# K as whole pairs in three shared slots in layers 1 and 2, and another order at a layer's end, in four attention layers of one decode step

## The chip, the cores and the metric

The kernel runs on one core of a Trainium2 chip. The metric is device time in microseconds, the median of several executions. A profile is one execution, taken by the hardware profiler, with its own time.

## What is computed

One token passes through four attention layers. Layers 1 and 3 use the weights and caches A, layers 2 and 4 those of B; everything is bfloat16.

```python
D, H, Sk, Dh = 640, 32, 8192, 192
def attn(x, k_cache, v_cache, wq, wo):
    q = (x @ wq) as [32 heads, 192]
    scores = einsum("hd,hkd->hk", q, k_cache) * Dh ** -0.5
    p = softmax(scores)
    o = einsum("hk,hkd->hd", p, v_cache)
    return o.reshape(1, 32 * 192) @ wo
x = x + attn(layernorm(x), A...)
x = x + attn(layernorm(x), B...)
x = x + attn(layernorm(x), A...)
x = x + attn(layernorm(x), B...)
```

K and V of one layer are 201 MB. Each byte is used for one query only, so nearly all of the 845 MB that are read are read once.

## The kernel before, in words

**Pairs, halves, slots.** In the code layers are counted 0 to 3; the text says layer 1 to 4. Heads go in 16 pairs (`NPAIR`). The K (or V) of a pair is 128 partitions x 24,576 values, 6144 KB, and consists of two halves of 12,288 values. `pool` in SBUF has eight slots (`NSLOT`), each as large as a half. Slots 5 to 7 (from `A_WQ`) hold A's query weights until layer 3. In layers 1 and 2 five slots are left: K's half 0 lies in slot 0, half 1 in slot 1, a pair's V in slots 2 and 3 as one transfer, and output weights, or a half of pair 15's K, in slot 4.

**Work on a pair.** `products` (L714) multiplies a K half in place by the query, which VectorE (DVE) does in chunks of columns (L729), and TensorE (PE) sums the products over the head dimension with matmuls by the identity, 24 a half, into a bank of `S` (one bank a half; L744, and L72 where the weights stay loaded). In layers 1 and 2 a half has two chunks of 96 columns for pairs 2 to 13, and four of 48 else. `softmax` (L778) reads both banks, `values` (L804) multiplies by V on PE (L841, L72), `gather` (L851) adds up the groups on DVE (L865, L867) and writes a row. The steps of a pair are m (half 0), m (half 1), s, v, e; every fifth pair also projects a block of output weights.

**Order.** `steps` is the order of work on the engines, `plan` the order of transfers. All large transfers are issued by SyncE (SP) in the order of `plan`, in one queue, on 16 DMA engines; each of them carries 8 of the 128 partitions, so a transfer has 16 landings, and the last one counts. `allot` (L345) gives a transfer its slots and notes in `before` whose work it waits for; `joint` lists the pairs that go as one transfer (`whole`, L242; issued at L464, others at L467). `transfer` (L426) waits on SyncE for the PE instruction after which the slots are free. What stands behind a waiting transfer waits too.

**A layer's end.** Pairs 14 and 15 come as halves. Pair 15's half 0 of K goes to slot 4 and half 1 to slot 0; then the last block of output weights into slot 4 (waits for that half 0), V15's first half into slot 1 and its second into slot 0, in layer 2 with its last part apart (`vq`) and two rows of weights apart (`wob`). In layer 1 the weights are issued before V15's halves too (`plan.insert(-2, ...)`, L302). The next layer's query weights take slots 2 to 4. Layer 3 starts with K in quarters (`kp`), the first of which waits for the projection of layer 2's last block.

Of the kernel before, what the change touches and what calls it, by code (L numbers as in the profile page):

```python
# [77 lines left out]
PAIRS_W = 5  # L78
# [4 lines left out]
def build(nc, A_x, A_k, A_v, A_wq, A_wo, B_x, B_k, B_v, B_wq, B_wo, out):  # L83
# [31 lines left out]
    with ExitStack() as ctx:  # L115
# [14 lines left out]
        K0Q = slot[NSLOT - 1][:, TS // 2:]  # L130
        QUARTER = [K0Q, slot[A_WQ - 1][:, TS // 2:], slot[A_WQ - 1][:, 0:TS // 2], slot[A_WQ][:, 0:TS // 2]]
        KEYS = [0, 2, 1, 3]
        CUT = NB[1] * D
        PIECE = [(0, TS // 2, K0Q), (TS // 2 + CUT, 3 * TS // 2, slot[A_WQ - 1][:, CUT:]),
                 (TS // 2, TS // 2 + CUT, slot[A_WQ - 1][:, 0:CUT]), (3 * TS // 2, 2 * TS, QUARTER[3])]
# [103 lines left out]
        def stays(kind, l, p):  # L239
            return l < 2 and (kind, pair(l, p)) in KEPT[l]  # L240

        def whole(kind, l, p):  # L242

            if l < 2:
                return (kind, l, p) in joint
            if kind == "k":
                return l == 3 and p > 1
            if p == NPAIR - 1:
                return False
            return l != 2 or p not in (0, PAIRS_W, 2 * PAIRS_W)  # L250
# [7 lines left out]
        for l in range(NL):  # L258
            if l < 3:
                plan += [("wq", l, 0), ("wq", l, 2)][:(1, 2, 0)[l]]  # L260
                ahead_of = [{0: (0, DC)}, {0: (0, DC - 1), 2: (DC - 1, DC)}, {0: (0, 1), 2: (1, DC)}][l]
                for c in ([0, 2, 3, 1, 4] if l == 2 else range(DC)):
                    steps += [("lead", l, 0, *ahead_of[c])] if c in ahead_of else []
                    steps.append(("r", l, c))
            else:
                both(("wq", l, 0))
            for p in range(NPAIR):
                if l == 0 and p == 0:
                    plan.append(("kh", l, p))
                if l == 2 and p == 0:  # L270
                    plan += [("kp", l, p, i) for i in range(1, len(PIECE))]
                else:
                    plan += [("k", l, p, u) for u in range(2)]
                if l == 2 and p == 0:
                    steps.append(("mq", l, p, 0))
                    for i in range(1, 4):
                        steps += [("mq", l, p, i), ("rd", l, p, i - 1)]
                    steps.append(("rd", l, p, 3))
                else:
                    steps.append(("m", l, p, 0))  # L280
                    if l == 2 and p == 1:
                        steps.append(("e", l, 0))
                    steps.append(("m", l, p, 1))
                if p == NPAIR - 1:
                    steps.append(("v", l, p - 1))
                steps.append(("s", l, p))
                if l == 3 and p == 0:
                    both(("wq", l, 1), ("wq", l, 2))
                if p < NPAIR - 2:
                    if first_load("v", l, p) == (l, p):  # L290
                        plan += [("v", l, p, u) for u in range(2)]
                    steps.append(("v", l, p))
                    if l != 2 or p > 0:
                        steps.append(("e", l, p))
                    if p + 1 in (PAIRS_W, 2 * PAIRS_W):
                        b = (p + 1) // PAIRS_W - 1
                        steps.append(("wc", l, b))
                        both(("wo", l, b))
            for i in (p - 1, p):
                if first_load("v", l, i) == (l, i):  # L300
                    plan += [("v", l, i, u) for u in range(2)]
            plan.insert(-2, ("wo", l, 2))  # L302
            steps += [("busy", l, 16), ("e", l, p - 1)] if NB[l] else [("e", l, p - 1)]
            steps += [("v", l, p, 0), ("wc", l, 2)] if NB[l] else [("wc", l, 2), ("v", l, p, 0)]
            steps += [("wo", l, 2), ("v", l, p, 1), ("e", l, p)]
            if NB[l]:
                plan.append(("vq", l))
                for i in range(len(WB[l])):
                    both(("wob", l, i))
            both(("wol", l))  # L310
            if l == 3:
                both(("woe", l))
# [32 lines left out]
        def allot(n):  # L345

            end = [-1 if h is None else released(h) for h in holder]

            def adjacent(k):
                i = min(range(0, NSLOT - k + 1, k), key=lambda i: max(end[i:i + k]))  # L350
                return list(range(i, i + k))

            if n[1] < 2:
                end15 = n[2] == NPAIR - 1
                if n[0] == "wq":
                    put([("wq", 1, g) for g in range(3)], [2, 3, 4])
                    before[n] += before["wq", 1, 1]
                elif n[0] == "wo":
                    put([n], [4])
                elif n[0] == "v" and not end15:  # L360
                    joint.add(n[:3])
                    put([n[:3] + (u,) for u in range(2)], [2, 3], True)
                elif n[0] == "v":
                    put([n], [1 - n[3]])
                else:
                    put([n], [(4, 0)[n[3]] if end15 else n[3]])
            elif n[0] == "v" and n[2] < NPAIR - 1 or n[0] == "k" and whole(*n[:3]):
                put([n[:3] + (u,) for u in range(2)], adjacent(2), whole(*n[:3]))
            else:
                put([n], adjacent(1))  # L370
# [33 lines left out]
        def wq_rows(l, g):  # L404

            c0, k = Q_PARTS[g]
            if l < 3:
                i = place[("wq", l % 2, 0)] * TS
                return pool[:, i + c0 * QW:i + (c0 + k) * QW].rearrange("p (c n) -> p c n", c=k)
            return slot[place[("wq", l, g)]][:, 0:k * QC[l]].rearrange("p (c n) -> p c n", c=k)  # L410

        def last_rows(l):

# [121 lines left out]
        def layer(l, ev_z, ev_true):  # L535
# [24 lines left out]

            if l < 3:
                ev_all = [need(("wq", l % 2, 0))] * (DC - 1) + [need(("wq", l % 2, 2 * (l % 2)))]
                every = pool[:, place[("wq", l % 2, 0)] * TS:][:, 0:DC * QW].rearrange("p (c n) -> p c n", c=DC)
            if l == 1:
                q0 = (ORDER[3]["q0"] + 1 - LEAD[3]) * PD
                for c0, k in Q_PARTS:
                    ev_first[c0] = DV.op(lambda v, c0=c0, k=k: v.tensor_copy(
                        wq0[:, c0:c0 + k, :], every[:, c0:c0 + k, q0:q0 + LEAD[3] * PD]), ev_all[c0])
            ev_q = {}

            def q_halves(p, *events, scale=None):
# [10 lines left out]
            def q_lead(p, c0=0, c1=DC):  # L582

                if l < 3:
                    x, w, ev = pair(l, p) * PD, every, ev_all[c0]
                else:
                    x, w, ev = (pair(l, p) - ORDER[l]["q0"] - 1 + LEAD[l]) * PD, wq0, ev_first[Q_PARTS[-1][0]]
                PE.wait(ev_xb, last["QB"], ev)
                for c in range(c0, c1):
                    e = PE.op(lambda t, c=c: t.matmul(  # L590
                        QM[:, 0:PD], lhsT=xb[:, c:c + 1].broadcast_to([P, P]), rhs=w[:, c, x:x + PD],
                        start=(c == 0), stop=(c == DC - 1)), signal=(c == c1 - 1), bank=QMu)
                if c1 == DC:
                    q_halves(p, e, ev_rs, scale=rs)
# [119 lines left out]
            def products(p, u):  # L714
# [6 lines left out]
                qi = (l * NPAIR + p) % 2  # L721
                DV.wait(need(nk), ev_q[p])
                chunks = []
                NC = 2 if l != 2 and 2 <= p < NPAIR - 2 else 4
                QD = DH // NC
                for c in range(NC):
                    d0 = c * QD
                    for kin, kout, n in parts:
                        e = DV.op(lambda v, d0=d0, kin=kin, kout=kout, n=n: v.tensor_tensor(  # L729
                            kout[:, :, d0:d0 + QD], kin[:, :, d0:d0 + QD],  # L730
                            q_sb[qi][:, d0:d0 + QD].unsqueeze(1).broadcast_to([P, n, QD]), ALU.mult))
                    chunks.append(e)
                last["q"][qi] = chunks[-1]
                S = SP_[u]
                PE.wait(last["S"][u], ev_const)
                for c in range(NC):
                    PE.wait(chunks[c])
                    for r in range(QD // R):
                        d0 = c * QD + r * R
                        fin = c == NC - 1 and r == QD // R - 1  # L740
                        held = PE.holds is ident
                        e = PE.op(lambda t, d0=d0, fin=fin, held=held: (
                            matmul_held(t, S[:, :], ident[:], k3[:, :, d0:d0 + R], d0 == 0, fin) if held else
# [149 lines left out]
            for n in [n for n in steps if n[1] == l]:  # L893
# [43 lines left out]
                else:  # L937
# [3 lines left out]
                        freed[("wo", l, 2)] = ev_y  # L941
                    if l == 1:
                        busy(1)
                following = 1 if n == ("mq", 2, 0, 2) or l == 3 and n[0] == "wq" else n[2] + 1 if n[0] == "m" and n[3] == 1 else NPAIR
                if following < NPAIR and following not in ev_q:
                    if following < LEAD[l]:
                        q_lead(following)
# [70 lines left out]
```

## Time and profile before

| What | us |
|---|---|
| median of 3 runs (1977.09 to 1979.3) | 1977.49 |
| the profiled execution | 1978.02 |
| its span, first to last instruction | 1976.0 |
| PE busy | 1301.7 |
| DVE busy | 1197.5 |
| ACT busy | 168.3 |
| DVE, products (L729) | 839.1 |
| PE, scores (L72, S) | 784.6 |

How to read it: the span is cut into 40 slices, and for each one the page gives tenths of busy time and what the DMA engines moved. HBM reads are 845.22 MB, 428 GB/s over the span. Issues are listed with the time from issue to landing: the 61 K halves of A's layers take 19.6 us (median), V pairs of B 28.2, so most of that time is spent in the queue. A row of a view by windows has: start and end, length, then busy time and number of instructions of PE, weight loads, DVE, ACT and POOL, the granted clock, the share of the DMA engines and GB/s. A row of the timeline has: start, length, engine, line, operation, out<-in, count, and in brackets the idle time before it and what ended it. SPq is SyncE's sequencer, where transfers are issued.

### The profile page before, as it was taken

The page shows a single profiled execution, that of the slowest core. Times are in us where ns is not written, and L with a number is a line of the kernel's source. Part 1 is how long each engine was busy: PE and PEld are TensorE (multiplying, and loading weights), DVE is VectorE, ACT ScalarE, POOL GpSimd, SP SyncE. Part 2 cuts the span into 40 slices and gives each one's busy share as a digit, 9 for nine tenths or more (in the row PEclk, how much of TensorE's full clock was granted, in tenths as well). Part 3 has the DMA queues.
Part 4 walks back from the last instruction along what each step waited for, and adds up shares of the span by engine and source line. Part 5 has one row for each costly group of instructions (what it writes and reads, how often), then busy time and mean ns, then how long its engine had stood idle before and what let it go on. Part 6 is the DMA issues. An engine that isn't in the chain of part 4 may idle for free.

```text
span 1976.0 us, 12053 instructions
## 1 busy us (share of the span) xinstructions
PE 1301.7 (66%) x7747; PEld 130.3 (7%) x2611; DVE 1197.5 (61%) x814; ACT 168.3 (9%) x529; POOL 4.6 (0%) x25
## 2 busy tenths in 40 slices
PE   4667576566566666576686665666666667657658
PEld 0000000000100000000020000000002001000001
DVE  3656556567257557566656565665764766665756
ACT  1000000000000000100010000000000100000000
POOL 0000000000000000000000000000000000000000
PEclk9777777788678778787787877878787878777778
DMA  9999999999999999999999999999999999999998
GB/s 414 429 429 432 431 430 435 427 431 430 433 429 433 432 429 435 426 431 434 426 398 435 427 425 432 432 430 431 432 431 427 435 430 434 434 434 431 431 430 370
DMA packets 30984, 845.99 MB, mean 428 GB/s; under 512 B 3538, under 2 KB 3668, under 8 KB 4564
## 3 DMA queue, kind: packets, MB, share of 16 engines
q1 hardware_dynamic: 30788, 845.23, 99.7%
q8 instruction: 40, 0.66, 0.1%
q14 instruction: 12, 0.10, 0.0%
q10 hardware_dynamic: 144, 0.00, 0.0%
HBM read 845.22 MB, written 0.00 MB: 428 GB/s over the span
## 4 chain that ended last, share of the span: by engine, by line
DMA 66%; PE 20%; DVE 12%; ACT 1%; issue 0%; SPq 0%; POOL 0%; ACTq 0%
DMA pool<-in_A_v_cache_dram 32%; DMA pool<-in_B_v_cache_dram 17%; DMA pool<-in_B_k_cache_dram 12%; DVE pool L729 8%; PE OY L72 7%; PE S L72 7%; PE OY L841 4%; DMA pool<-in_A_k_cache_dram 4%; DMA pool<-in_B_wq_dram 1%; DVE OY L865 1%; DVE acc L867 1%; DVE s_sb L784 1%; DVE pool L758 1%; PE OY L679 0%; PE S L744 0%
## 5 line engine op out<-in xcount | busy, mean ns | idle before, releaser
L729 DVE TENSOR_TENSOR pool<-pool,q_sb 128x3072 bf16<-128x3072 bf16 (+2 forms) x364 | 839.1, 2368 | 106.4 <-DMA pool<-in_B_k_cache_dram 56.6
L72 PE MATMUL S<-pool,ident 128*128 128x512 bf16 x3004 | 784.6, 423 | 24.6 <-DVE pool L729 22.6
L865 DVE TENSOR_TENSOR OY<-OY,small 128x1536 f32<-128x1536 f32 x60 | 106.0, 1766 | 306.6 <-PE OY L72 306.4
L72 PE MATMUL OY<-pool,p_sb 128*16 128x512 bf16 x1920 | 224.7, 559 | 0.0
L841 PE MATMUL OY<-pool,p_sb 128*16 128x512 bf16 (+1 forms) x1216 | 155.6, 535 | 80.6 <-DMA pool<-in_A_v_cache_dram 55.2
L879 PE MATMUL TB<-acc,small 128*33 128x192 f32 x120 | 46.7, 488 | 208.2 <-DVE acc L867 208.2
L784 DVE TENSOR_REDUCE s_sb<-S 128x128 f32<-128x1024 f32 x63 | 77.2, 1225 | 153.1 <-PE S L72 153.1
L744 PE MATMUL S<-pool,ident 128*128 128x512 bf16 x66 | 37.7, 571 | 146.1 <-DVE pool L729 146.1
L579 ACT ACTIVATE q_sb<-QM 64x192 bf16<-64x192 f32 x118 | 38.3, 324 | 862.6 <-PE QM L631 861.9
L867 DVE TENSOR_REDUCE acc<-OY 128x192 f32<-128x1536 f32 x60 | 105.4, 1757 | 2.0
L888 ACT ACTIVATE rows<-TB,small 1x192 bf16<-1x192 f32 x120 | 49.4, 412 | 643.9 <-PE TB L879 642.4
L799 ACT ACTIVATE p_sb<-s_sb,small 64x128 bf16<-64x128 f32 x128 | 55.7, 435 | 168.5 <-DVE small L793 167.7
L789 PE MATMUL QM<-ident,m_bf 128*64 128x64 bf16 x128 | 14.0, 216 | 82.6 <-DVE m_bf L786 82.6
L855 DVE RECIPROCAL small<-TB 33x2 f32<-33x2 f32 x64 | 11.2, 175 | 90.8 <-PE TB L814 73.0
L814 PE MATMUL TB<-small,ones 128*33 128x2 f32 x120 | 14.2, 188 | 74.1 <-ACT p_sb L799 74.1
L841 PEld LDWEIGHTS OY<-pool,p_sb 128*16 128x16 bf16 (+1 forms) x1216 | 37.2, 113 | 252.9 <-issue 160.6
L631 PEld LDWEIGHTS QM<-rows,one_b 1*128 1x128 bf16 x59 | 5.4, 91 | 733.3 <-issue 733.3
L679 PE MATMUL OY<-pool,oT 128*1 128x320 bf16 x330 | 38.6, 411 | 2.2 <-ACT oT L709 2.2
L793 DVE TENSOR_REDUCE small<-QM 128x1 f32<-128x64 f32 x64 | 14.4, 225 | 30.6 <-PE QM L789 30.6
L879 PEld LDWEIGHTS TB<-acc,small 128*33 128x33 f32 x120 | 10.4, 134 | 312.5 <-DVE acc L867 312.5
L799 ACT ACTIVATION_READ_ACCUMULATOR p_sb<-s_sb,small 64x1 f32 x128 | 23.3, 182 | 0.0
L860 DVE TENSOR_SCALAR acc<-OY,small 128x192 f32<-128x192 f32 x4 | 1.7, 418 | 32.7 <-PE OY L841 32.7
(87 smaller groups left out, 254.2 us busy)
## 6 DMA issues: line engine op xcount, KB each, us to landing
pool<-in_A_k_cache_dram SPq DMA_DIRECT2D x61, 3072.0 KB, 19.6
pool<-in_B_v_cache_dram SPq DMA_DIRECT2D x28, 6144.0 KB, 28.2
pool<-in_A_v_cache_dram SPq DMA_DIRECT2D x27, 6144.0 KB, 24.6
pool<-in_B_k_cache_dram SPq DMA_DIRECT2D x36, 3072.0 KB, 19.3
pool<-in_B_k_cache_dram SPq DMA_DIRECT2D x14, 6144.0 KB, 41.0
pool<-in_A_v_cache_dram SPq DMA_DIRECT2D x10, 3072.0 KB, 14.3
pool<-in_A_wo_dram SPq DMA_DIRECT2D x6, 2400.0 KB, 16.8
pool<-in_B_wo_dram SPq DMA_DIRECT2D x4, 2400.0 KB, 31.1
```

The lines of the kernel that those rows point to most:

```text
L72: return t.add_instruction(mybir.InstMatmult(name=t.bass.get_next_instruction_name(), engine=mybir.EngineType.PE, ins=[t.lower_ap(rhs), t. ...
L579: lambda a, h=h, r=r, f=f: a.activation(q_sb[i][r, :], QM[r, h * DH:(h + 1) * DH], ACT.Copy, scale=f),
L679: e = PE.op(lambda t, i=i, h=h, f=l < 3 and n[2] == 0 and i == 0, fin=n == last_row and i == k - 1: t.matmul(YR[32 * h:32 * h + 1, :], lhs ...
L729: e = DV.op(lambda v, d0=d0, kin=kin, kout=kout, n=n: v.tensor_tensor(kout[:, :, d0:d0 + QD], kin[:, :, d0:d0 + QD], q_sb[qi][:, d0:d0 + Q ...
L744: t.matmul(S[:, :], lhsT=ident[:], rhs=k3[:, :, d0:d0 + R], start=d0 == 0, stop=fin)),
L784: lambda v: v.tensor_reduce(s[:], S_[:].rearrange("p (j r) -> p j r", r=R), AX.X, ALU.add),
L799: ev_p[p] = AC.op(lambda a, h=h, r=r: a.activation(p_sb[par][r, :, h], s[r, :], ACT.Exp, bias=negm[par][r, 0:1], accum_out=l_col[par][r, h ...
L841: t.matmul(o, lhsT=x, rhs=y, start=f, stop=fin) if c == 0 else
L865: e = DV.op(lambda v: v.tensor_tensor(o3, o3, pick[:, 0:VK].unsqueeze(2).broadcast_to([P, VK, DH]), ALU.mult), bank=Ou)
L867: e = DV.op(lambda v: v.tensor_reduce(acc[:], O.rearrange("p (i d) -> p d i", d=DH), AX.X, ALU.add), e, bank=Ou)
L879: e = PE.op(lambda t: t.matmul(TB[64:97, C_O:C_O + DH], lhsT=half33, rhs=acc[:], start=True, stop=True), bank=TBu)
L888: last["TO"] = last["row_written"] = AC.op(lambda a, h=h: a.activation(orow[:, o0 + h * DH:o0 + (h + 1) * DH], TB[64 + 32 * h:65 + 32 * h, ...
```

## The change

**Three slots.** In layers 1 and 2, V's pairs and B's query weights move to slots 0 and 1. K takes slots 2, 3 and 4 (`RING` is 2). For pairs 1 to 13, K is one transfer of 6144 KB into two neighbouring slots (`KPOS`): slots 3 and 4 for pair 1, then in turn 2 and 3, and 3 and 4. Slot 3 is in both, and its half is worked off first (`units`): half 0 where the pair lies in 3 and 4, half 1 where it lies in 2 and 3 (pairs 2, 4, 5, 7, 9, 10, 12). The next pair's transfer waits for that first half, and for the half before it in the other slot, which is long done. At pairs 5 and 10 the slots stay the same, since output weights lie in slot 4.

**Chunks.** Products of these pairs go in chunks of 96, 64 and 32 columns.

**A layer's end.** The slots are mirrored: pair 14's halves in 2 and 3, pair 15's in 4 and 2, V15's first half in 3 and its second in 2. In layers 1 and 2 the last output weights are issued between V15's halves; layers 3 and 4 keep their order.

**Query weights.** They are read by their part's slot (`wq_rows`), no more as one stretch of three slots.

```diff
+        RING = A_WQ - 3
+        KPOS = {}
+        for p in range(1, NPAIR - 2):
+            KPOS[p] = RING + 1 if p == 1 else KPOS[p - 1] if p % PAIRS_W == 0 else 2 * RING + 1 - KPOS[p - 1]
...
+        def units(l, p):
+
+            return (1, 0) if l < 2 and p in KPOS and KPOS[p] == RING else (0, 1)
...
-                    steps.append(("m", l, p, 0))
+                    steps.append(("m", l, p, units(l, p)[0]))
                     if l == 2 and p == 1:
                         steps.append(("e", l, 0))
-                    steps.append(("m", l, p, 1))
+                    steps.append(("m", l, p, units(l, p)[1]))
...
-            plan.insert(-2, ("wo", l, 2))
+            plan.insert(-1 if l < 2 else -2, ("wo", l, 2))
...
                 if n[0] == "wq":
-                    put([("wq", 1, g) for g in range(3)], [2, 3, 4])
+                    put([("wq", 1, g) for g in range(3)], [0, 1, RING + 2])
                     before[n] += before["wq", 1, 1]
                 elif n[0] == "wo":
-                    put([n], [4])
+                    put([n], [RING + 2])
                 elif n[0] == "v" and not end15:
                     joint.add(n[:3])
-                    put([n[:3] + (u,) for u in range(2)], [2, 3], True)
+                    put([n[:3] + (u,) for u in range(2)], [0, 1], True)
                 elif n[0] == "v":
-                    put([n], [1 - n[3]])
+                    put([n], [RING + 1 - n[3]])
+                elif n[2] in KPOS:
+                    joint.add(n[:3])
+                    put([n[:3] + (u,) for u in range(2)], [KPOS[n[2]], KPOS[n[2]] + 1], True)
                 else:
-                    put([n], [(4, 0)[n[3]] if end15 else n[3]])
+                    put([n], [RING + (2 - 2 * n[3] if end15 else n[3])])
...
             c0, k = Q_PARTS[g]
-            if l < 3:
-                i = place[("wq", l % 2, 0)] * TS
-                return pool[:, i + c0 * QW:i + (c0 + k) * QW].rearrange("p (c n) -> p c n", c=k)
-            return slot[place[("wq", l, g)]][:, 0:k * QC[l]].rearrange("p (c n) -> p c n", c=k)
+            l, w = (l % 2, QW) if l < 3 else (l, QC[l])
+            return slot[place["wq", l, g]][:, 0:k * w].rearrange("p (c n) -> p c n", c=k)
...
-                NC = 2 if l != 2 and 2 <= p < NPAIR - 2 else 4
-                QD = DH // NC
-                for c in range(NC):
-                    d0 = c * QD
+                cuts = [DH // 2, DH // 3, DH // 6] if l < 2 and p in KPOS else [DH // 2] * 2 if l != 2 and 2 <= p < NPAIR - 2 else [DH // 4] * 4
+                for c, QD in enumerate(cuts):
+                    d0 = sum(cuts[:c])
...
-                for c in range(NC):
+                for c, QD in enumerate(cuts):
                     PE.wait(chunks[c])
                     for r in range(QD // R):
-                        d0 = c * QD + r * R
-                        fin = c == NC - 1 and r == QD // R - 1
+                        d0 = sum(cuts[:c]) + r * R
+                        fin = d0 + R == DH
```

More of the change, by code (lines that the diff above doesn't have):

```diff
@@ L562, in layer @@
                 ev_all = [need(("wq", l % 2, 0))] * (DC - 1) + [need(("wq", l % 2, 2 * (l % 2)))]
-                every = pool[:, place[("wq", l % 2, 0)] * TS:][:, 0:DC * QW].rearrange("p (c n) -> p c n", c=DC)
             if l == 1:
                 q0 = (ORDER[3]["q0"] + 1 - LEAD[3]) * PD
-                for c0, k in Q_PARTS:
-                    ev_first[c0] = DV.op(lambda v, c0=c0, k=k: v.tensor_copy(
-                        wq0[:, c0:c0 + k, :], every[:, c0:c0 + k, q0:q0 + LEAD[3] * PD]), ev_all[c0])
+                for g, (c0, k) in enumerate(Q_PARTS):
+                    ev_first[c0] = DV.op(lambda v, g=g, c0=c0, k=k: v.tensor_copy(
+                        wq0[:, c0:c0 + k, :], wq_rows(1, g)[:, :, q0:q0 + LEAD[3] * PD]), ev_all[c0])
             ev_q = {}
@@ L584, in q_lead @@
                 if l < 3:
-                    x, w, ev = pair(l, p) * PD, every, ev_all[c0]
+                    x, w, ev = pair(l, p) * PD, [wq_rows(l, c // 2)[:, c % 2, :] for c in range(DC)], ev_all[c0]
                 else:
-                    x, w, ev = (pair(l, p) - ORDER[l]["q0"] - 1 + LEAD[l]) * PD, wq0, ev_first[Q_PARTS[-1][0]]
+                    x, ev = (pair(l, p) - ORDER[l]["q0"] - 1 + LEAD[l]) * PD, ev_first[Q_PARTS[-1][0]]
+                    w = [wq0[:, c, :] for c in range(DC)]
                 PE.wait(ev_xb, last["QB"], ev)
@@ L590, in q_lead @@
                     e = PE.op(lambda t, c=c: t.matmul(
-                        QM[:, 0:PD], lhsT=xb[:, c:c + 1].broadcast_to([P, P]), rhs=w[:, c, x:x + PD],
+                        QM[:, 0:PD], lhsT=xb[:, c:c + 1].broadcast_to([P, P]), rhs=w[c][:, x:x + PD],
                         start=(c == 0), stop=(c == DC - 1)), signal=(c == c1 - 1), bank=QMu)
@@ L723, in products @@
                 chunks = []
-                NC = 2 if l != 2 and 2 <= p < NPAIR - 2 else 4
-                QD = DH // NC
-                for c in range(NC):
-                    d0 = c * QD
+                cuts = [DH // 2, DH // 3, DH // 6] if l < 2 and p in KPOS else [DH // 2] * 2 if l != 2 and 2 <= p < NPAIR - 2 else [DH // 4] * 4
+                for c, QD in enumerate(cuts):
+                    d0 = sum(cuts[:c])
                     for kin, kout, n in parts:
-                        e = DV.op(lambda v, d0=d0, kin=kin, kout=kout, n=n: v.tensor_tensor(
+                        e = DV.op(lambda v, d0=d0, QD=QD, kin=kin, kout=kout, n=n: v.tensor_tensor(
                             kout[:, :, d0:d0 + QD], kin[:, :, d0:d0 + QD],
@@ L943, in layer @@
                         busy(1)
-                following = 1 if n == ("mq", 2, 0, 2) or l == 3 and n[0] == "wq" else n[2] + 1 if n[0] == "m" and n[3] == 1 else NPAIR
+                following = 1 if n == ("mq", 2, 0, 2) or l == 3 and n[0] == "wq" else n[2] + 1 if n[0] == "m" and n[3] == units(l, n[2])[1] else NPAIR
                 if following < NPAIR and following not in ev_q:
```

## The prediction

> **What bounds the kernel now.** I read the page first: the share of the DMA queue, the slices, the chain that ended last.
>
> ```profile
> span 1976.0 us, 12053 instructions
> ...
> DMA  9999999999999999999999999999999999999998
> GB/s 414 429 429 432 431 430 435 427 431 430 433 429 433 432 429 435 426 431 434 426 398 435 427 425 432 432 430 431 432 431 427 435 430 434 434 434 431 431 430 370
> ...
> q1 hardware_dynamic: 30788, 845.23, 99.7%
> ...
> DMA 66%; PE 20%; DVE 12%; ACT 1%; issue 0%; SPq 0%; POOL 0%; ACTq 0%
> ```
>
> SyncE's one queue fills 99.7% of the 16 DMA engines' time, and PE and DVE are busy for 66% and 61%. Their shares of the chain are pieces after which a transfer is issued, not pieces in which the engines stand still. So I went to the DMA engines' own records. Each engine carries 8 of a transfer's 128 rows, one packet a row. A 24,576-byte packet takes 915 ns (median), one of 49,152 bytes 1820 ns, the closing semaphore write 9 ns. From one transfer's last landing to the next one's I subtracted eight such packets: over the whole run 5.4 us are left over, of which 2.25 stand at one place (V of pair 0, layer 3) and most of the rest comes in steps near 1 us, where a 16 KB instruction fetch (936 to 1107 ns) delays the slowest engine. Only the slowest engine counts: the first of the 16 lands up to 5.2 us before it.
>
> The stages, with DMA share and GB/s last on each line:
>
> ```profile
> 56.00:480.00 424.00, 279.11 (x1515) 21.21 (x410) 268.82 (x153) 34.71 (x114) 0.00 (x0) 0.78 1.00 431
> 560.00:960.00 400.00, 261.25 (x1479) 22.73 (x427) 245.46 (x136) 32.70 (x107) 0.00 (x0) 0.78 1.00 431
> 1560.00:1930.00 370.00, 242.76 (x1423) 21.50 (x430) 235.15 (x134) 31.34 (x104) 0.00 (x0) 0.77 1.00 432
> ```
>
> Layers 1 and 2 (K in halves) move 431 GB/s and layer 4 (K whole) 432, all at a share of 1.00. There is hardly anything to gain but packet size, and much to lose if the queue runs dry.
>
> **The change, part by part.**
>
> *K of pairs 1 to 13, layers 1 and 2, as one transfer.* Before, a pair's K costs each engine 2 x (8 x 0.915 + 0.009) = 14.658 us; after, 8 x 1.820 + 0.009 = 14.569. That is 0.089 us less, for 26 pairs 2.3 us. A second way: undisturbed periods (V landing to V landing) are 29.14 us in layers 1 and 2 and 29.06 in layer 4, 0.08 x 26 = 2.1. With mean instead of median packets (917 and 1820 ns) it is 2.9. I take **-2.3**, bounds -2.1 and -2.9.
>
> By the Trainium skill ("DMA: Bandwidth & Descriptors", Anatomy of one DMA) a DMA costs about 2.0 us fixed beside its bytes; were that paid in series, 26 fewer would save 52 us and the time would be about 1925 (an estimate from that page). The trace disagrees for a filled queue, by the row that follows.
>
> K halves that stand one behind the other land 7.29 to 7.31 us apart where eight packets and the write make 7.33, so no start of a transfer shows.
>
> *What the whole transfer takes from the queue's lead.* Call the last landing of a pair's K T. Before, half 0 was worked on while half 1 still came, so after T only one half was left. V was issued thus:
>
> ```profile
> 223.49 5.76 SPq L467 DMA_DIRECT2D pool<-in_A_k_cache_dram  x2
> 237.75 0.33 SPq L464 DMA_DIRECT2D pool<-in_A_v_cache_dram  x1
> 252.99 5.51 SPq L467 DMA_DIRECT2D pool<-in_A_k_cache_dram  x2
> ```
>
> At 237.75 the K before it was due to land last at 247.84: 10.1 us in hand. After, both halves start at T. The nearest row is layer 4, which works off whole pairs already:
>
> ```profile
> 1740.74 13.17 DVE L729 TENSOR_TENSOR pool<-pool,q_sb 128x6144 bf16<-128x6144 bf16 x4 [1.82 <-DMA pool<-in_B_k_cache_dram]
> ...
> 1757.16 1.23 DVE L784 TENSOR_REDUCE s_sb<-S 128x128 f32<-128x1024 f32 x1 [3.26 <-PE S L72]
> ...
> 1765.87 0.33 SPq L464 DMA_DIRECT2D pool<-in_B_k_cache_dram  x1
> ```
>
> K landed at 1740.71; the products took until 1753.9, the score matmuls until 1757.1, softmax and the V matmuls until 1765.87, where V's slots came free: T + 25.1 (two more such pairs: 25.2 from 1682.58, 24.7 from 1806.17). The change cuts a half's products into 96, 64 and 32 of 192 columns instead of 96 and 96. The last 12 matmuls after the last product took some 3.2 us there. With 24 matmuls at 0.23 us (a row of 12 takes 2.76) after the second half's first product, at T + 10.0 with 0.4 for the handover, PE ends at T + 15.9 instead of 16.4. V's next issue is then **T + 24.6**. The next K lands last at T + 29.06, so 4.4 us are in hand where it was 10.1. A dry engine gets its first packet of a new transfer 2.0 to 2.9 us after the issue (issues at 964.62, 987.55, 1019.11, 1176.02; the worst, two gaps in one, 3.6 at 1023.25). On the slowest engine 4.4 covers all of them: **0**. The engines that lead by up to 5.2 us will run dry, which only takes their lead. Without the cover each microsecond of lateness costs 1 us in each of 20 exposed pairs (per layer, V after pairs 1 to 12 without 4 and 9, where output weights of 5.75 us stand in the queue too).
>
> The next K needs only the slot that was worked off first: T + 3.4 + 0.4 + 24 x 0.23 = T + 9.3, while V lands last at T + 14.57: 5.3 in hand. K of pairs 5 and 10 reuses the same two slots, so it waits for both halves, T + 15.9, against V and the output weights until T + 14.57 + 5.75 = 20.3: 4.4. K of pair 1 waits for the second half of pair 0: in layer 2 at 550.76 instead of 544.24, with V landing last at about 557: 6.2. Behind it on SyncE stands only V of pair 1, issued at 561.90 before. All three: 0.
>
> *Instructions.* 24 x 2 products more and 2 x 2 fewer, 44 on DVE. Products of 3072 columns take 1.68 us and of 6144 3.29, so cutting costs under 0.1 us a pair. What hides it is DVE's pause: its last gather ends 3.6 us after V's issue, at T + 28.2, and the next K lands at T + 29.06. Without that cover it is 0.1 x 26 = 2.6 us. 41 fetches for 12,053 instructions make 44 more 0.15 of a fetch: 0 to 1 us, taken as 0. PE's count, and the other order of halves (14 pairs), add nothing: a softmax reads both banks together.
>
> *Layer ends.* V15's first half goes to SyncE before the output weights. Before, it stood behind their wait:
>
> ```profile
> 987.55 0.33 SPq L480 DMA_DIRECT2D pool<-in_B_wo_dram  x1
> 987.92 0.43 SPq L467 DMA_DIRECT2D pool<-in_B_v_cache_dram  x1
> 993.64 0.33 SPq L460 DMA_DIRECT2D pool<-in_B_v_cache_dram  x1
> ```
>
> It waits for pair 14's second half alone, whose scores are done at 976.67, so 11 us sooner; the weights then come at 987.55 into a queue that lasts to 992.74 + 7.33 = 1000.1. The gap of 988.2 to 989.8 closes. It held 6 of 16 engines, 0.33 us over all; the slowest was not among them (V14's last landing is 992.74, the weights' 3.46 later, as their packets take). So 0, and -0.33 at most, with slow first packets about -0.9. What follows (V15's second half, last rows, layer 3's K pieces) has the same order and bytes. The 2.25 us at V of layer 3 hang on pair 15's landing, projection, norm and query rows, which don't move. In layer 1 nothing was dry.
>
> **Sum.** -2.3 + 0 + 0: span 1973.7. The profiled execution took 1978.02 (1976.0 and 2.0 around it), so 1975.7; the median of the runs, 1977.49, lies 0.53 below that: **1975.2 us**, -0.12%. A measurement of this kernel tells about 0.2% (4 us) from no change.
>
> **Rivals.**
>
> 1. *Nothing net.* Engines that lead run dry in each of the 20 pairs and lose their lead, so that fetches (18 in layers 1 and 2) meet engines with none in hand. For: leads of 5.2 us exceed 4.4. Against: 4.4 less 2.0 to 2.9 leaves a lead of 1.5 to 2.4, over a fetch's 1.05. Two fetches that now show eat the gain: 1977.3.
>
> 2. *V comes too late; slower.* Place: SyncE's V issue after the V matmuls. It decides once T + 24.6 becomes over T + 29.06 - 3.6 = 25.5. For: only 0.9 us separate the two at the worst refill. Against: layer 4's rows lie within 24.7 to 25.2 at a granted clock of 0.77 (0.78 in layers 1 and 2), and four of the five refills took 2.9 or less. At T + 26.0, 0.5 us x 20 = 10, less 2.3: 1985.2.
>
> 3. *The layer ends pay.* The output weights' projection, at 1006.6 to 1008.6 before, ends some 3 us sooner and layer 3's first K piece is issued sooner; if the 2.25 us went with the 0.9, 1975.2 - 3.15 = 1972.0. Against: the later pieces wait for landings that keep their place.
>
> 4. *Each start of a transfer is exposed*, 1.01 us (the run's first, issue to first packet), 26 of them: 1977.5 - 26.3 = 1951. Against it stand the 7.3 us between halves. [...]
>
> **How the numbers follow.** Forecast 0.58, of which 0.03 falls under 1973.5 with a lucky placing of fetches; rival 1 0.14; rival 2 0.15, of which 0.01 stays inside 0.2%; rival 3 0.12; rival 4 0.01. Faster by over 0.2% (below 1973.5): 0.03 + 0.12 + 0.01 = 0.16. Slower (above 1981.4): 0.14. Within: 0.70. Range: rival 3 to the lower end, with 0.2 below it for means in place of medians, 1971.8; above, to a V late by 0.36 us x 20 (1975.2 + 7.3), 1982.5. Outside lie about 0.05 and 0.12.
>
> **What would show it.** Right: K transfers of 6144 KB, V landings 29.06 us apart in layers 1 and 2, V issues some 24.6 us after K's last landing, DMA share 1.00, no gap at 988, the gap at V of layer 3 as before. Wrong: V landings over 29.2 apart, PE and DVE waiting for V, or layer 2's end shorter by over 1 us.

## The result and the profile after

The changed kernel takes 1992.45 us (median of 6 runs, 1987.17 to 1995.91), the kernel before 1977.34 beside it: a ratio of 1.0075, 95% interval 1.0064 to 1.0086. It is slower by 15 us. The profiled execution took 1993.62 us, 15.6 more than that of before.

The page of the changed kernel, the lines that were shown of before:

```profile
span 1991.7 us, 12071 instructions
...
DMA  9999999999999999999999999999999999999998
GB/s 411 434 417 417 423 423 428 402 427 428 429 432 414 427 423 401 423 425 427 429 416 432 432 429 432 434 427 429 439 423 426 436 435 433 429 435 432 430 435 368
...
q1 hardware_dynamic: 27044, 845.23, 99.3%
...
DMA 60%; PE 22%; DVE 16%; ACT 1%; issue 0%; SPq 0%; POOL 0%; ACTq 0%
DMA pool<-in_B_k_cache_dram 26%; DMA pool<-in_A_k_cache_dram 18%; PE S L72 15%; DMA pool<-in_A_v_cache_dram 14%; DVE pool L737 13%; PE OY L72 3%; PE OY L849 2%; DMA pool<-in_B_wo_dram 2%; DVE OY L873 1%; DVE acc L875 1%; PE S L752 1%; DMA pool<-in_B_v_cache_dram 1%; DVE s_sb L792 1%; DVE pool L766 1%; ACT p_sb L807 0%
```

There are 3744 packets fewer, as 26 larger transfers must give (26 x 144, semaphore writes included). The loss lies in the first half of the run, where most slices have 401 to 428 GB/s. The second line of the chain has turned over. Of before it was:

```profile
DMA pool<-in_A_v_cache_dram 32%; DMA pool<-in_B_v_cache_dram 17%; DMA pool<-in_B_k_cache_dram 12%; DVE pool L729 8%; PE OY L72 7%; PE S L72 7%; PE OY L841 4%; DMA pool<-in_A_k_cache_dram 4%; DMA pool<-in_B_wq_dram 1%; DVE OY L865 1%; DVE acc L867 1%; DVE s_sb L784 1%; DVE pool L758 1%; PE OY L679 0%; PE S L744 0%
```

It was led by V transfers (32% and 17%), and is now led by K transfers (26% and 18%), with the score matmuls (S, 15%) and the products (L737, 13%) between them.

The same three stages by windows (length, busy times, then granted clock, DMA share, GB/s):

```profile
56.00:480.00 424.00, 261.84 (x1484) 20.26 (x407) 260.64 (x167) 33.12 (x108) 0.00 (x0) 0.77 0.99 421
560.00:960.00 400.00, 240.23 (x1411) 21.45 (x421) 237.95 (x154) 32.71 (x107) 0.00 (x0) 0.76 0.99 420
1560.00:1930.00 370.00, 243.54 (x1439) 21.36 (x427) 237.59 (x138) 31.70 (x105) 0.00 (x0) 0.79 1.00 432
```

Layers 1 and 2 went from 431 to 421 and 420 GB/s, and layer 4 is unchanged. The DMA share is still 0.99: it does not show the loss, and why is told below.

The chain of the changed kernel in order of time, pairs 4 to 7 of layer 1 (start, length, what):

```profile
137.51 19.28 DMA pool<-in_A_k_cache_dram
156.79 0.02 issue
156.82 3.37 DVE pool L737
...
160.84 12.64 PE S L72 x47
...
173.50 19.68 DMA pool<-in_A_k_cache_dram
193.18 0.02 issue
193.21 3.37 DVE pool L737
196.58 0.05 issue
196.62 0.61 PE S L752
197.23 6.36 PE S L72 x23
203.58 0.02 issue
203.60 18.66 DMA pool<-in_A_k_cache_dram
...
222.28 3.37 DVE pool L737
225.66 0.05 issue
225.70 0.61 PE S L752
226.31 7.17 PE S L72 x23
233.47 0.02 issue
233.49 18.25 DMA pool<-in_A_k_cache_dram
```

This is a closed loop: K lands (193.18), the first half's products and 24 matmuls run, the next K is issued (203.60), it lands (222.26). V's issue is not in it; V is there only as the packets behind which K waits in the queue. An issue comes 10.4 or 11.2 us after the landing, for pair 5 (173.50) 16.7 us after, as it waits for both halves; from issue to landing it takes 18.3 to 19.7 us, where its packets take 14.57.

The landing records give the time in hand, that is the time from an issue to the last landing of the transfer ahead of it, and what is left over of a transfer's last-to-last landing when its packets are subtracted. Pair 4's K (issued at 137.51) had 2.9 us in hand and 1.8 left over, pair 5's 3.5 and 1.6, pair 6's (203.60) 4.1 and 0.0. The leftover of the whole run went from 5.4 to 23.8 us, 18.4 more. The 28 K transfers behind a transfer of another kind in layers 1 and 2 (pair 1 of layer 1 is left out, see the table below) have 18.7 more (19.7, before 1.0), so elsewhere it is slightly less. 18.4 less the 2.3 for larger packets is 16.1; 15.6 was measured.

### The profile page after: what moved, and what is told of

Read it like the earlier page. It is cut to its first block, busy times and chain, and to the rows that moved or that the text cites. A ratio compares the mean times of both kernels' runs of the same rounds, so it can differ in the third digit from the quotient of the medians.

```text
span 1991.7 us, 12071 instructions
## 1 busy us (share of the span) xinstructions
PE 1274.9 (64%) x7747; PEld 128.0 (6%) x2611; DVE 1201.3 (60%) x858; ACT 168.5 (8%) x529; POOL 4.6 (0%) x25
## 4 chain that ended last, share of the span: by engine, by line
DMA 60%; PE 22%; DVE 16%; ACT 1%; issue 0%; SPq 0%; POOL 0%; ACTq 0%
DMA pool<-in_B_k_cache_dram 26%; DMA pool<-in_A_k_cache_dram 18%; PE S L72 15%; DMA pool<-in_A_v_cache_dram 14%; DVE pool L737 13%; PE OY L72 3%; PE OY L849 2%; DMA pool<-in_B_wo_dram 2%; DVE OY L873 1%; DVE acc L875 1%; PE S L752 1%; DMA pool<-in_B_v_cache_dram 1%; DVE s_sb L792 1%; DVE pool L766 1%; ACT p_sb L807 0%
## 5 line engine op out<-in xcount | busy, mean ns | idle before, releaser
L737 DVE TENSOR_TENSOR pool<-pool,q_sb 128x3072 bf16<-128x3072 bf16 (+4 forms) x408 | 841.1, 2129 | 181.0 <-DMA pool<-in_B_k_cache_dram 98.3
L72 PE MATMUL OY<-pool,p_sb 128*16 128x512 bf16 x1920 | 206.8, 519 | 0.0
L849 PE MATMUL OY<-pool,p_sb 128*16 128x512 bf16 (+1 forms) x1216 | 144.1, 497 | 44.3 <-DMA pool<-in_A_v_cache_dram 36.2
L863 DVE RECIPROCAL small<-TB 33x2 f32<-33x2 f32 x64 | 11.2, 175 | 89.7 <-PE TB L822 73.3
L822 PE MATMUL TB<-small,ones 128*33 128x2 f32 x120 | 14.6, 192 | 74.1 <-ACT p_sb L807 74.1
L752 PEld LDWEIGHTS S<-pool,ident 128*128 128x128 bf16 x66 | 6.8, 103 | 273.5 <-DVE pool L737 272.4
## 6 DMA issues: line engine op xcount, KB each, us to landing
pool<-in_B_k_cache_dram SPq DMA_DIRECT2D x10, 3072.0 KB, 18.7
pool<-in_A_wo_dram SPq DMA_DIRECT2D x6, 2400.0 KB, 18.3
```

Source lines behind the costliest of these rows:

```text
L72: return t.add_instruction(mybir.InstMatmult(name=t.bass.get_next_instruction_name(), engine=mybir.EngineType.PE, ins=[t.lower_ap(rhs), t. ...
L737: e = DV.op(lambda v, d0=d0, QD=QD, kin=kin, kout=kout, n=n: v.tensor_tensor(kout[:, :, d0:d0 + QD], kin[:, :, d0:d0 + QD], q_sb[qi][:, d0 ...
L752: t.matmul(S[:, :], lhsT=ident[:], rhs=k3[:, :, d0:d0 + R], start=d0 == 0, stop=fin)),
L849: t.matmul(o, lhsT=x, rhs=y, start=f, stop=fin) if c == 0 else
```

## The experiments

The theory (A): the next pair's K is issued too late, because its transfer waits for a half whose work begins only when the whole pair has landed; the DMA queue then has too little in hand. The rivals: (B) packets of 48 KB into these slots are slow at a transfer's start whenever they are issued; (C) the new slots, chunks or the layer's end cost the time.

**Early halves.** K of pairs 1 to 13 as two transfers again, in the same three slots, the half for the long free slot first.

```diff
-            return (1, 0) if l < 2 and p in KPOS and KPOS[p] == RING else (0, 1)
+            return (1, 0) if l < 2 and p in KPOS and KPOS[p] != RING else (0, 1)
...
-                    plan += [("k", l, p, u) for u in range(2)]
+                    plan += [("k", l, p, u) for u in units(l, p)]
...
-                    joint.add(n[:3])
-                    put([n[:3] + (u,) for u in range(2)], [KPOS[n[2]], KPOS[n[2]] + 1], True)
+                    put([n[:3] + (u,) for u in range(2)], [KPOS[n[2]], KPOS[n[2]] + 1])
```

> The changed kernel with K of pairs 1 to 13 as two halves again, in the same three slots; the half for the slot that has long been free is issued and worked off first, so the queue holds 7.3 us more when the shared slot's half is issued. Theory A (the next K is issued too late, 2.9 to 4.4 us before the queue ends): the loss goes, 1976 to 1979, no first packets over nominal. Theory B (packets of 48 KB in these slots are slow at a transfer's start whenever they are issued): the same, 1976 to 1979, so this run alone does not tell A from B. Theory C (the new slots, chunks of 96/64/32 or the layer ends cost the time): stays at 1988 to 1994.

Measured: 1976.27 us, ratio 0.9994 (0.9984 to 1.0004). The slots, the chunks of 96, 64 and 32 and both layer ends are in it, and it is as fast as before: C falls.

**Late halves.** Two transfers, issued where the whole one was, and worked off when both have landed.

```diff
-                    joint.add(n[:3])
...
-                DV.wait(need(nk), ev_q[p])
+                DV.wait(*[need(("k", l, p, i)) for i in (range(2) if l < 2 and p in KPOS else [u])], ev_q[p])
```

> The changed kernel with K of pairs 1 to 13 as two halves, but both issued at the moment at which the whole transfer was, and worked off only when both have landed. Theory A: the lateness is the same, so the loss stays, plus 2.3 us for the smaller packets, less up to 5 us if a slow first packet is half as dear at half the size: 1988 to 1996. Theory B: 1976 to 1980.

Measured: 1994.76 us, ratio 1.0088 (1.0072 to 1.0103). Packets of 24 KB lose about as much as those of 48 KB when they are issued as late: B falls. From the first two runs together, it is the moment of the issue.

**Fine chunks on the first half.** Transfers, slots and order stay; the half that is worked off first has four chunks of 48 columns, so that PE starts on it sooner.

```diff
-                cuts = [DH // 2, DH // 3, DH // 6] if l < 2 and p in KPOS else ...
+                cuts = ([DH // 4] * 4 if u == units(l, p)[0] else [DH // 2, DH // 3, DH // 6]) if l < 2 and p in KPOS else ...
```

> The changed kernel with the products of the half that is worked off first in four chunks of 48 columns, so PE starts on it 1.6 us after K's landing instead of 3.4. Theory A: the next K is issued up to 1.6 us sooner (after 8.6 to 10 us instead of 10.2 to 11.6), 4.5 to 6 us are in hand, and most of the loss goes but that of pairs 5 and 10 (6 us): 1981 to 1986. Theory B and C: 1990 to 1994.

Measured: 1974.71 us, ratio 0.9990 (0.9981 to 1.0000). This change of one line takes the whole loss away, 18 us, which no other theory allows. The size was a miss: I had left 6 us for pairs 5 and 10. The timeline of this run at pair 10:

```profile
306.37 13.37 DVE L737 TENSOR_TENSOR pool<-pool,q_sb 128x3072 bf16<-128x3072 bf16 x7 [1.42 <-DMA pool<-in_A_k_cache_dram]
...
308.18 0.61 PE L752 MATMUL S<-pool,ident 128*128 128x512 bf16 x1 [2.42 <-DVE pool L737]
308.58 6.80 PE L72 MATMUL S<-pool,ident 128*128 128x512 bf16 x23
316.45 5.34 PE L72 MATMUL S<-pool,ident 128*128 128x512 bf16 x24 [1.07 <-DVE pool L737]
...
321.83 0.33 SPq L473 DMA_DIRECT2D pool<-in_A_k_cache_dram  x1
```

PE starts 1.8 us after the products do, not 3.4; it is done with the first half before the second half's first product, and so both halves end 15.5 us after the products' start instead of 16.6. The K transfers of pairs 5 and 10 have 4.8 to 5.1 us in hand instead of 3.5 to 4.3, and that suffices.

**The layer's end alone.** The kernel before with the last output weights behind V15's first half.

```diff
-            plan.insert(-2, ("wo", l, 2))
+            plan.insert(-1 if l < 2 else -2, ("wo", l, 2))
```

> The kernel before with the last output weights of layers 1 and 2 behind V15's first half, and nothing else. Theory A and B: 1976 to 1978 (the gap at 988 closes on engines that lead, at best 0.9 us). Theory C, as far as the layer ends are meant: 1981 or more.

Measured: 1976.02 us, ratio 0.9995 (0.9986 to 1.0005): nothing that can be told from no change.

**The same again.** The fine chunks once more, in more rounds.

> The same as e3_fine_first, once more and beside more runs of the kernel before: theory A says that its 4.5 to 6.2 us in hand suffice and that the 2.3 us of the larger packets stay: 1973.5 to 1976, ratio 0.9985 to 0.9995. If the 1974.7 was luck of the chip: 1976 to 1979.

Measured: 1975.66 us, ratio 0.9997 (0.9988 to 1.0005). The loss is gone again, and the gain of the larger packets is at the limit of what can be told; the time in hand goes down to 4.5 us in both runs, and 4.0 us are left over at K transfers, where the first had 1.2.

**Still finer.** 24, 40, 64 and 64 columns on the first half.

```diff
+                cuts = ([24, 40, 64, 64] if u == units(l, p)[0] else [DH // 2, DH // 3, DH // 6]) if l < 2 and p in KPOS else ...
```

> The first half's products in chunks of 24, 40, 64 and 64 columns, so PE starts 0.8 us after K's landing. Theory A with its point at about 4.5 us in hand: nothing more to gain than the few tenths that fall below it in e3 (K transfers of 4.5 to 4.8 us in hand): 1973 to 1975.5. If the loss goes on falling with the time in hand beyond 4.5 us, some 1 to 2 us less than e3 beside it.

Measured: 1974.14 us, ratio 0.9989 (0.9980 to 0.9997): faster than both kernels. It is also 1.5 us less than the fine chunks beside it, as the other branch of the expectation said (a loss that goes on falling beyond 4.5 us), so this run does not decide between the two. In the landing records the difference lies in K transfers during which an instruction fetch is on record: 4.0 us are left over in the repeat, 0.6 here. By windows its layers 1 and 2 are:

```profile
56.00:480.00 424.00, 273.45 (x1514) 20.67 (x410) 272.33 (x188) 34.76 (x114) 0.00 (x0) 0.79 1.00 432
560.00:960.00 400.00, 262.47 (x1478) 22.18 (x423) 250.57 (x172) 32.73 (x107) 0.00 (x0) 0.78 1.00 431
```

**Coarse.** 128, 32 and 32 columns on the first half, so PE starts later.

```diff
+                cuts = ([128, 32, 32] if u == units(l, p)[0] else [DH // 2, DH // 3, DH // 6]) if l < 2 and p in KPOS else ...
```

> The first half's products in chunks of 128, 32 and 32 columns, so PE starts 1.1 us later than in the changed kernel, and the next K is issued up to 1.1 us later: 1.8 to 3.3 us in hand. Theory A: 0.5 to 1.1 us more per pair, 26 pairs: 2005 to 2022. Without a point near 4.5 us (a cost by packets, places or ends): 1990 to 1994.

Measured: 2008.07 us, ratio 1.0164 (1.0148 to 1.0180), in the lower part of what A said (the profiled execution is the fastest of four, 2002.88).

**Two slots.** K of pairs 1 to 13 always in slots 2 and 3.

```diff
-            KPOS[p] = RING + 1 if p == 1 else KPOS[p - 1] if p % PAIRS_W == 0 else 2 * RING + 1 - KPOS[p - 1]
+            KPOS[p] = RING
```

> The changed kernel with K of pairs 1 to 13 always in slots 2 and 3, so each transfer waits for both halves of the pair before, 16 to 16.7 us after its landing, when the queue has been empty for 1.5 to 2 us. Theory A: 22 pairs lose 4.5 + 1.8 us each where they lost 0.7: 2080 to 2125.

Measured: 2081.53 us, ratio 1.0530 (1.0511 to 1.0549), at the lower edge of what A said. The third slot is worth some 90 us. Layer 1 by windows; the DMA share shows a queue that is really empty:

```profile
56.00:480.00 424.00, 230.87 (x1348) 18.87 (x381) 233.43 (x148) 30.67 (x100) 0.00 (x0) 0.74 0.90 384
```

Taken together, from the landing records of the profiled executions, K transfers that stand behind a transfer of another kind in layers 1 and 2 (28 a run; pair 1 of layer 1 is left out, as it leaves 0.7 to 1.4 us in every kernel):

| Kernel | in hand, median us | left over, sum us | this execution, us |
|---|---|---|---|
| early halves (first half) | 23.6 | 0.8 | 1977.4 |
| before (first half) | 10.9 | 1.0 | 1978.0 |
| finest first | 5.8 | 0.6 | 1973.9 |
| fine first | 5.4 | 1.2 | 1974.2 |
| fine first, again | 5.2 | 4.0 | 1975.4 |
| late halves (first half) | 3.9 | 14.6 | 1993.0 |
| changed | 3.7 | 19.7 | 1993.6 |
| coarse first | 2.9 | 26.3 | 2002.9 |
| two slots | -1.3 | 102.0 | 2080.3 |

The point lies near 4.5 us. Above it, in the runs with fine and finest chunks, what is left over comes in single steps of 0.2 to 1.2 us, and a 16 KB instruction fetch is on record during each of these 18 transfers (during the 66 others, 22 times). Below it most transfers leave something, but not all: in the changed kernel three with 3.8 to 4.1 us in hand leave nothing.

## Why the prediction was wrong

- *K as one transfer, -2.3 us*: right. Where nothing is late, V landings are 29.05 to 29.07 us apart (finest and fine first) against 29.13 to 29.15 before, and the finest first is 2.4 us below the runs of the kernel before beside it.
- *V's issue at T + 24.6, 4.4 us in hand*: right in size. It was 21.7 to 25.4 after the landing, with 4.1 us in hand at the least and 6.6 as the median; V transfers lose little. The sign for being wrong came: V landings were up to 31.1 us apart where no weights lay between.
- *The next K at T + 9.3, 5.3 in hand, cost 0*: this step failed, first in its term. I took 24 matmuls at 0.23 us, from a row of 12. They take 6.97 us in the chain at 197, 7.78 at 226, so 0.29 and 0.32 each, and the issue came at T + 10.2 to 11.6. The granted clock varies by pair: 0.84 there at 193 to 204, 0.64 at 222 to 234:

```profile
222.26:234.00 11.74, 8.30 (x28) 0.10 (x1) 11.71 (x5) 0.00 (x0) 0.00 (x0) 0.64 0.93 402
...
193.20:203.60 10.40, 6.98 (x25) 0.10 (x1) 10.39 (x5) 0.00 (x0) 0.00 (x0) 0.84 1.04 449
```

- *A dry engine is served 2.0 to 2.9 us after the issue, so 4.4 covers it*: this bound failed too, and all three zeroes hung on it. It was read from engines that were dry, and it held for them; the engine that decides still had work and was served later. After the issue at 359.43, fifteen engines start their first packet 1.0 to 1.6 us later, and it takes 2.0 to 2.7 us in place of 1.82. Counted from its end less 1.82, it came 1.6 to 2.1 us after the issue. The sixteenth first packet starts 3.6 us after the issue, 1.1 after the last packet of V has ended, and takes 2.6: by the same count it came after 4.4 us, and from it the packets lead on to the last landing. In six of the nine K transfers with under 3.3 us in hand this count is 4.1 to 4.6 us. Over layers 1 and 2 the first packets of the K transfers are 10.2 us over nominal, averaged over the engines; before, first packets were at nominal. So some 4.5 us are needed, and 2.9 to 4.6 were there. By these figures either error alone would have cost little: 5.3 in hand is more than 4.5, and 2.9 in hand still meets a bound of 2.9.
- *One such place stood in the trace of before*: V at 1023.25 had 2.4 us in hand and left 2.25 over, 4.6 together, as the late K transfers have it now (4.6 to 4.9 where V is ahead and over 1 us is left). The prediction took it for two gaps in one, 3.6, and did not carry its price over.
- *Pairs 5 and 10 at T + 15.9, 4.4 in hand*: T + 16.0 to 16.7, 3.5 to 4.3 in hand, 6.0 us left over in four transfers. The mechanism was named, its cost was mis-sized by the same bound.
- *Rival 2* was nearest, with the wrong place: it watched V, which waits for a whole pair's work but has a whole K ahead of it. K waits for half a pair's work but has only what remains of V ahead. Its price, 1 us a pair for each us of lateness, was too high: coarse first has 0.8 us less in hand as the median (22 us for 26 pairs) and takes 16 us more by the medians of the runs, 9 by the profiled executions; two slots has 5.1 less (132 us) and takes 87 more.
- *The layer's end, 0*: right, by the run that has it alone. *Rival 3* did not come. *Rival 1* did not cost the 15 us, but its mechanism shows: with some 5 us in hand the engines' lead shrank (first to last landing 1.7 to 2.9 us in fine first, in place of up to 5.2), and K transfers left 1.2 us over in fine first and 4.0 in its repeat, most of it while a fetch was on record, where before they left 1.0. *Rival 4* would have set the early halves and the fine chunks, with 26 transfers fewer, apart by 26 us; they differ by 1.6. The 41 fetches of the prediction are 40 on the page; nothing hangs on it.

## What to carry to other kernels

Making a transfer larger moves two moments: when its data can be worked on, and when its successor can be issued; work out the time that the queue still holds at each issue, with the slowest rate that the engine's rows show, and not the best. Measure the lead that a queue needs from transfers that were late, by their landings, as a first packet that takes longer is counted as busy all the while. If the lead is short by a microsecond, a finer first step of the work that frees the buffer can give it back: here 24 columns first in place of 96 turned a loss of 15 us into a gain of 2.4 against runs of the kernel before beside it.

## What was not expected of the hardware

With a DMA share of 0.99, layers 1 and 2 moved 421 and 420 GB/s instead of 431: the longer first packets (10.2 us over nominal) count as busy, and whether they wait or move slowly the records don't tell. Into a queue that had been empty for 0.7 to 2.4 us (two slots), a K transfer lands 16.8 to 18.5 us after its issue, so the refill costs 2.3 to 3.9 us beside the 14.57 of its packets. A queue about to run dry needs a longer lead than that: the K of 137.51 found work for 2.9 us and yet landed 19.28 us after its issue, 4.7 beside its packets, of which 2.9 were the work ahead and 1.8 were lost. Why the engine that is still busy is served later than the dry ones, and why first packets are slow, stays open; that late halves lose about as much shows only that it isn't the packet's size.
